# Two attention sweeps woven into two recurrent chains, in a hand-written order

## The chip, the cores and the metric

The kernel runs on one NeuronCore of a Trainium2 chip. The engines are TensorE (PE, with its weight loads PEld), VectorE (DVE), ScalarE (ACT), GpSimd (POOL) and SyncE (SP, which here only issues DMAs). The metric is the device time of one execution in microseconds (us): the median of several runs.

## The reference, cut to what matters

The kernel computes the forward pass and all gradients of a gated sum of two branches for 2048 tokens of width 576.

```python
g = sigmoid((x * gate_w).sum(-1))
out = g * A(x) + (1 - g) * B(x_B)          # and the gradients of out . grad_out

# A: 32 query heads of 18, one key head, full softmax over 2048 x 2048
p = softmax(q_h @ k.T * 18**-0.5); o_h = p @ v;  A = concat(o_h) @ wo

# B: 64 segments of 32 tokens, 32 heads of 128; 8 memory rows go from segment to segment
for s in range(64):
    h = concat(mem, x[32*s:32*s+32])        # 40 rows
    q, k, v = h @ Wq, h @ Wk, h @ Wv
    o = masked_softmax(q @ k.T * 128**-0.5) @ v
    o = o @ Wo
    mem, out_s = o[:8], o[8:]
```

Branch A has no order among its blocks. Branch B's memory rows are a recurrence: 64 steps forward, and 64 steps backward for the gradient.

## The kernel before, in words

The kernel is written in a tile framework: pools hand out buffers ("bufs" is how many a name has), every semaphore is derived from the tiles read and written, and a scheduler orders the instructions by priority. Everything is unrolled. The stages follow each other as `build_full` calls them.

- `prep`, `a_weights`, `a_setup`: gate, transposes of x and of the incoming gradient, branch A's keys and values (tiles KV, VK, WK).
- `a_pass1`, **sweep 1**: for 16 pairs of heads by 4 blocks of 512 queries it makes QD (queries and output gradients of both heads, in the four 32-row strips of one tile; `a_qd`), then runs over 16 key tiles. Per key tile: four matmuls of 32 rows give two scores (a_S) and two dP products (a_dP), ACT takes two exponentials (L947), DVE multiplies both heads' dP by E in one instruction of 1024 columns (L948), and four matmuls with 64 columns of weights add E and W into a_acc. `a_post` normalises a block and keeps its rows of output and dq in SBUF.
- `a_pass2`, **sweep 2**: the same products with keys along the free axis, for 4 blocks of 512 keys by 16 pairs by 16 query tiles; b_acc collects dk and dv with four matmuls of 32 columns each for E and dS.
- `a_out`: branch A's output projection.
- `b_proj_x`: q, k and v of all 2048 tokens, 16 tiles by 3 weights, kept in DRAM as rows and transposed.
- `b_chain_fwd`, **forward chain**: 64 segments. Each projects 8 memory rows with Wk, Wq, Wv (20 matmuls a half of a weight, in four column strips), transposes them, forms the memory rows' scores (c_sm), takes the softmax, multiplies by v (po), and forms the next memory rows with 160 matmuls of 8 columns (c_pm).
- `make_transposed_weights`, then `b_bulk`: everything of B that does not feed the recurrence, 16 token tiles by 8 groups of four heads: scores, softmax, output, dO (five matmuls with WoT and four transposes), dP, dS, dq.
- `b_chain_bwd`, **backward chain**: 64 segments in reverse: dO of the memory rows (r_pj), dS, the gradients of q, k, v (r_pkv, r_pdq), their product with three transposed weights (r_ph, 192 matmuls) and a last reduction to the memory rows' gradient (r_sm, L627).
- `b_post`, `b_mem_tok`, `b_dw`, `a_final`: remaining gradients.

Helpers at L61 to L71 (`evac`, `mm`, `tr`) record all copies out of PSUM, matmuls and transposes, so tiles tell more than lines here. Most DMAs are issued by SP; those of `dq_eng` alternate between SP and POOL.

Of the kernel before, what the change touches and what calls it, by code (L numbers as in the profile page):

```python
# [11 lines left out]
P = 128  # L12

D = 576
# [16 lines left out]
class Kern:  # L31
# [50 lines left out]
    def setup_B_dram(self, dram):  # L82
# [12 lines left out]
        self.xTd = {w: t(w + "xT_dram", [NTT, P, HB, P]) for w in ("q", "k", "v")}  # L95
        self.mTd = {w: t(w + "mT_dram", [NTT, P, HB, 32]) for w in ("k", "v")}
# [6 lines left out]
        self.dsmq_dram = t("dsmq_dram", [NSEG, MEM, HB, 32])  # L103
        self.dmT_dram = t("dmT_dram", [P, NKT, NSEG, MEM])
# [3 lines left out]
    def setup_B_consts(self, pool):  # L108
# [17 lines left out]
        mx = pool.tile([P, 2, 160], BF16, name="maskX")  # L126
        nc.gpsimd.memset(mx[:], 0.0)
        for j in range(2):
            nc.gpsimd.affine_select(out=mx[:, j, 0:128], in_=mx[:, j, 0:128], compare_op=ALU.is_ge, fill=NEGB,
                                    base=0, pattern=[[-1, P]], channel_multiplier=1)  # L130
            nc.gpsimd.memset(mx[:, j, 128:160], NEGB)
            for sl in range(4):
                r = slice(32 * sl, 32 * sl + 32)
                if sl:
                    nc.gpsimd.memset(mx[r, j, 0:32 * sl], NEGB)
                nc.gpsimd.memset(mx[r, j, 128 + 8 * sl:136 + 8 * sl], 0.0)
        self.maskX = mx
# [38 lines left out]
    def b_proj_x(self, sp, psum):  # L176
        nc = self.nc
        for tt in range(self.NTT):
            xt = sp.tile([P, NKT, P], BF16, name="p_x", bufs=2)
            nc.sync.dma_start(xt[:], self.xT_dram[:, :, tt * P:(tt + 1) * P].rearrange("k p t -> p k t"))  # L180
            for w in ("q", "k", "v"):
                tok = sp.tile([P, J], BF16, name="p_tok", bufs=2)
                for jc in range(8):
                    pb = psum.tile([P, 512], F32, name="p_pb", bufs=4)
                    for kt in range(NKT):
                        rows = KT_ROWS[kt]
                        self.mm(pb[:], lhsT=xt[0:rows, kt, :], rhs=self.W[w][0:rows, kt, jc * 512:(jc + 1) * 512],
                                start=(kt == 0), stop=(kt == NKT - 1))
                    self.evac(tok[:, jc * 512:(jc + 1) * 512], pb[:])
                nc.sync.dma_start(self.xtok[w][tt * P:(tt + 1) * P, :], tok[:])  # L190
                tT = sp.tile([P, HB, P], BF16, name="p_tT", bufs=2)
                for h8 in range(4):
                    pt = psum.tile([P, 8, P], BF16, name="p_pt", bufs=2)
                    for i in range(8):
                        h = 8 * h8 + i
                        self.tr(pt[:, i, :], tok[:, h * E:(h + 1) * E], P)
                    self.evac(tT[:, 8 * h8:8 * h8 + 8, :], pt[:])
                nc.sync.dma_start(self.xTd[w][tt], tT[:])
# [7 lines left out]

    def b_chain_fwd(self, keep, sp, psum):
        nc = self.nc
        NSEG = self.NSEG
        hist = keep.tile([P, NKT, NSEG, MEM], BF16, name="memT")  # L210
# [6 lines left out]
        for s in range(NSEG):  # L217
            tt, sl = s // 4, s % 4
            h_ = hm[s % 2]
            kx = sp.tile([P, HB, 32], BF16, name="c_kx", bufs=2)  # L220
            nc.gpsimd.dma_start(kx[:], self.xTd["k"][tt][:, :, 32 * sl:32 * sl + 32])
# [4 lines left out]
            nc.gpsimd.tensor_copy(hist[:, 0:4, s, :], h_[:, 0:4, 0:8])  # L226
            nc.gpsimd.tensor_copy(hist[0:64, 4, s, :], h_[0:64, 4, 0:8])
            if sl == 0:
                mT = {w: sp.tile([P, 4, 8, 4, 8], BF16, name=f"c_{w}mT", bufs=1) for w in ("k", "v")}
            tm = {}  # L230
            for w in ("k", "q", "v"):
                t2 = sp.tile([P, 8, E], BF16, name=f"c_{w}2", bufs=2)
                for j in range(2):
                    pj = psum.tile([P, 512], F32, name="c_pj", bufs=3)
                    for kt in range(NKT):
                        rows = KT_ROWS[kt]
                        for c in range(4):
                            self.mm(pj[32 * c:32 * c + 32, :], lhsT=h_[0:rows, kt, :],
                                    rhs=self.W[w][0:rows, kt, c * 1024 + j * 512:c * 1024 + (j + 1) * 512],
                                    start=(kt == 0), stop=(kt == NKT - 1), tp=(0, 32 * c))  # L240
                    self.evac(t2[:, 4 * j:4 * j + 4, :].rearrange("p u e -> p (u e)"), pj[:])
                tm[w] = t2
                for c in range(4):
                    nc.sync.dma_start(self.mtok[w][s * 8:(s + 1) * 8, c * 1024:(c + 1) * 1024], self.m_rows(t2, c))
                pt = psum.tile([P, 8, P], BF16, name="c_pt", bufs=2)
                for u in range(8):
                    self.tr(pt[:, u, :], t2[:, u, :], P)
                src = pt[:].rearrange("p u (c t) -> p u c t", t=32)[:, :, :, 0:8]
                if w == "q":
# [1033 lines left out]
```

## Time and profile before

| what | value |
|---|---|
| median of 3 runs | 11392.89 us (11385.8 to 11398.63) |
| profiled execution, its own time | 11406.79 us |
| span in the profile | 11405.0 us |
| PE busy | 8865.9 us, 78% |
| DVE, ACT, POOL busy | 36%, 31%, 14% |
| mean granted PE clock | 0.725 |

A span is from the first to the last instruction. "Busy" is the time in which an engine had an instruction; PE's ends are modelled, and a busy PE is not PE at its peak. The granted clock is the share of full speed at which the throttle lets PE run. In the timeline the columns are start, length, engine, line, operation, output<-inputs, shape and count, and in brackets the idle time before and what ended it. In groups by line or tile: count, then either busy time and mean ns, or shortest, median and longest ns.

### The profile page before, as it was taken

The numbers are of one execution on the slowest core, as the hardware profiler recorded it, in microseconds if no ns is written. First come the engines' busy times: TensorE is split into PE (matmuls) and PEld (weight loads), VectorE is DVE, ScalarE is ACT, GpSimd is POOL, SyncE is SP. The second block draws the span as 40 slices with busy tenths as digits, with TensorE's granted clock in tenths as the row PEclk, the third lists the DMA queues.
The fourth block names the chain that finished last, engine by engine and source line by source line (L and its number), as shares of the span: only waits on it lengthen the run. The fifth ranks groups of instructions, "written<-read, shape, count | busy, mean of one in ns | idle before, by whom it ended". The sixth has DMA issues, their size and how long they took to land. (4 is left out here: it accounts for less than half of the span.)

```text
span 11405.0 us, 219104 instructions
## 1 busy us (share of the span) xinstructions
PE 8865.9 (78%) x91009; PEld 3869.9 (34%) x91416; DVE 4143.1 (36%) x5742; ACT 3592.5 (31%) x6629; POOL 1540.5 (14%) x2664
## 2 busy tenths in 40 slices
PE   6777777799999998888876666665777776655898
PEld 2222222211112444444443333333333333333344
DVE  5666666688886331212122222221111111111001
ACT  4666666677776331111121111110000001112000
POOL 2111111100000000000022222221111111112101
PEclk8888888655556997777755655666666668877999
DMA  1000000311112442222254444444222224445544
GB/s 66 9 9 9 9 9 9 96 49 49 46 49 85 175 172 43 44 44 43 43 164 114 111 118 114 111 117 121 55 55 54 55 60 125 124 116 188 169 149 137
DMA packets 929961, 945.24 MB, mean 83 GB/s; under 512 B 457193, under 2 KB 801458, under 8 KB 910146
## 3 DMA queue, kind: packets, MB, share of 16 engines
q1 hardware_dynamic: 859330, 714.18, 21.7%
q0 software_dynamic: 69632, 217.01, 6.9%
q8 instruction: 716, 11.73, 0.4%
q14 instruction: 283, 2.32, 0.1%
HBM read 558.16 MB, written 372.57 MB: 82 GB/s over the span
## 5 line engine op out<-in xcount | busy, mean ns | idle before, releaser
L948 DVE TENSOR_TENSOR a_W<-a_dP,a_E 128x1024 bf16<-128x1024 f32 x1024 | 1252.4, 1225 | 583.3 <-ACT a_E L947 483.8
L1035 DVE TENSOR_TENSOR b_dS<-b_dP,b_E 128x1024 bf16<-128x1024 f32 x1024 | 1231.3, 1223 | 211.3 <-PE b_S L66 163.1
L947 ACT ACTIVATE a_E<-a_S 128x512 bf16<-128x512 f32 x2048 | 1116.0, 595 | 445.8 <-PE a_S L66 385.6
L1034 ACT ACTIVATE b_E<-b_S 128x512 bf16<-128x512 f32 x2048 | 1111.1, 594 | 351.0 <-DVE b_dS L1035 243.2
L66 PE MATMUL b_S<-b_KV,b_QD 32*128 32x512 bf16 x2048 | 897.8, 588 | 25.0 <-DMA b_QD<-qd_dram 25.0
L66 PE MATMUL a_acc<-a_W,a_WK 128*64 128x512 bf16 x2048 | 471.0, 447 | 387.5 <-DVE a_W L948 387.1
L66 PE MATMUL b_acc<-b_E,b_SD 128*32 128x512 bf16 x2048 | 626.9, 608 | 4.3 <-DMA b_SD<-sd_dram 3.3
L66 PE MATMUL b_acc<-b_dS,b_SD 128*32 128x512 bf16 x2048 | 626.2, 607 | 4.3 <-DVE b_dS L1035 1.8
L66 PE MATMUL b_dP<-b_KV,b_QD 32*128 32x512 bf16 x2048 | 620.7, 603 | 0.0
L66 PE MATMUL r_ph<-WT,r_dT 128*32 128x512 bf16 x12288 | 562.0, 353 | 29.5 <-ACT r_dT L608 29.5
L66 PE MATMUL a_S<-a_QD,a_KV 32*128 32x512 bf16 x2048 | 539.4, 443 | 44.6 <-ACT a_QD L922 43.1
L66 PE MATMUL w_acc<-w_d,w_h 128*128 128x512 bf16 (+1 forms) x2352 | 523.1, 380 | 37.5 <-DMA w_d<-dqx_dram 34.8
L66 PE MATMUL a_acc<-a_E,a_VK 128*64 128x512 bf16 x2048 | 520.2, 441 | 28.9 <-ACT a_E L947 25.8
L679 DVE COPY y_T<-y_pt 128x512 bf16<-128x512 bf16 x384 | 151.3, 422 | 934.8 <-PE y_pt L71 920.5
L66 PE MATMUL a_dP<-a_QD,a_KV 32*128 32x512 bf16 x2048 | 455.6, 441 | 0.0
L66 PE MATMUL y_pdx<-WT,y_T 128*128 128x64 bf16 (+1 forms) x2976 | 426.5, 289 | 24.1 <-ACT y_dx L685 10.9
L66 PEld LDWEIGHTS <-a_WK 128*64 128x64 bf16 x2048 | 195.1, 111 | 687.5 <-issue 680.0
L66 PE MATMUL c_pm<-c_oT,WoN 128*128 128x8 bf16 (+1 forms) x10080 | 340.3, 173 | 38.4 <-DVE c_oT L282 27.0
L66 PEld LDWEIGHTS <-r_dT 128*32 128x32 bf16 x12288 | 256.4, 109 | 334.9 <-issue 217.6
L66 PEld LDWEIGHTS <-b_SD 128*32 128x32 bf16 x4096 | 120.6, 101 | 731.1 <-issue 725.5
L66 PEld LDWEIGHTS <-WoN 128*128 128x128 bf16 (+1 forms) x10080 | 338.1, 114 | 50.9 <-issue 49.6
L66 PE MATMUL y_pk<-y_qB,y_dsB 128*128 128x512 bf16 x112 | 49.9, 446 | 391.9 <-DMA y_dsB<-dsmq_dram 391.9
(424 smaller groups left out, 13336.7 us busy)
## 6 DMA issues: line engine op xcount, KB each, us to landing
b_SD<-sd_dram SPq DMA_DIRECT2D x64, 512.0 KB
b_QD<-qd_dram SPq DMA_DIRECT2D x64, 512.0 KB
qx_dram<-p_tok SPq DMA_DIRECT2D x16, 1024.0 KB
qxT_dram<-p_tT SPq DMA_DIRECT2D x16, 1024.0 KB
kx_dram<-p_tok SPq DMA_DIRECT2D x16, 1024.0 KB
kxT_dram<-p_tT SPq DMA_DIRECT2D x16, 1024.0 KB
vx_dram<-p_tok SPq DMA_DIRECT2D x16, 1024.0 KB
vxT_dram<-p_tT SPq DMA_DIRECT2D x16, 1024.0 KB
```

Of the source, the lines that this page charges most:

```text
L66: return self.nc.tensor.matmul(out, lhsT, rhs, start=start, stop=stop, tile_position=tp, skip_group_check=True)
L679: nc.vector.tensor_copy(tT[:], pt[:])
L947: nc.scalar.activation(Et[:, i, :], S[i][:, :], ACT.Exp, scale=SCALEA)
L948: nc.vector.tensor_tensor(out=Wt[:], in0=dP[:], in1=Et[:], op=ALU.mult)
L1034: nc.scalar.activation(Et[:, i, :], S[i][:, :], ACT.Exp, scale=SCALEA)
L1035: nc.vector.tensor_tensor(out=dS[:], in0=dP[:], in1=Et[:], op=ALU.mult)
```

## The change

Both sweeps and both chains become generators. `weave` runs one piece of a chain and then two half-steps of a sweep, with a context in which the written order is kept on every engine. A half-step is one head's share of a key tile: 2048 in each sweep. Sweep 1 goes with the forward chain, sweep 2 with the backward chain.

Inside the sweeps, scores run two half-steps ahead of their use, and the DVE product is 512 columns wide. QD is made by `a_qd_all` ahead of the weave and read back from DRAM block by block, as are KV, VK and WK. `a_post` is cut into steps, uses the chain's PSUM slot and writes its rows to DRAM at once. The chains' copies out of PSUM after projections are all ACT's, the transposed copies DVE's; their loads are issued by SP a segment ahead; c_x and r_x are single PSUM slots shared by the chain's small products; the backward product r_ph is cut into two halves of 288 columns. dO of the tokens moves from `b_bulk` into `b_proj_x`, which `b_bulk` then loads, and WoT is made earlier. The memory rows go to DRAM in each segment and are turned to token order in `b_mem_tok`.

The core of the diff:

```diff
+    def weave(self, chain, sweep, per_piece):
+        with self.tc.manual_schedule():
+            for _ in chain:
+                for _ in range(per_piece):
+                    next(sweep, None)
+            for _ in sweep:
+                pass
 ...
-    def b_proj_x(self, sp, psum):
+    def b_proj_x(self, ws, srcT, sp, psum):
 ...
-            for w in ("q", "k", "v"):
+            for w in ws:
+                Wt = self.WoT if w == "dO" else self.W[w]
 ...
+    def proj_mem(self, st, Wt, j, psum, tag):
+        pj = psum.tile([P, 512], F32, name=tag, bufs=2)
+        for kt in range(NKT):
+            rows = KT_ROWS[kt]
+            for c in range(4):
+                self.mm(pj[32 * c:32 * c + 32, :], lhsT=st[0:rows, kt, :],
+                        rhs=Wt[0:rows, kt, c * 1024 + j * 512:c * 1024 + (j + 1) * 512],
+                        start=(kt == 0), stop=(kt == NKT - 1), tp=(0, 32 * c))
+        return pj
 ...
     def b_chain_fwd(self, keep, sp, psum):
+            nxt = load(s + 1)
+            for w in ("k", "q"):
                 for j in range(2):
+                    pj = self.proj_mem(h_, self.W[w], j, psum, "c_pj")
+                    self.evac(flat(t2[w], j), pj[:], use="s")
+                    yield
+            src = self.mem_T(t2["k"], psum, "c_x", 1)
+            mT_out("k", src)
+            rows_out("k")
+            yield
+            pj = self.proj_mem(h_, self.W["v"], 0, psum, "c_pj")
 ...
+            ps = psum.tile([P, P], F32, name="c_x", bufs=1)
 ...
             nc.scalar.activation(Et[:].rearrange("p a b -> p (a b)"), ps[:], ACT.Exp, scale=SCALEB)
+            yield
+            src = self.mem_T(t2["v"], psum, "c_pj", 2)
+            mT_out("v", src)
+            yield
+            den = psum.tile([P, 64], F32, name="c_x", bufs=1)
 ...
             self.expand(PB[:], pn[:].rearrange("p a (u q) -> p (a u) q", q=8), 16)
+            yield
+            yield
+            po = psum.tile([P, 8, 32], F32, name="c_x", bufs=1)
 ...
+            yield
             if s + 1 < NSEG:
+                pm = psum.tile([P, NKT, 8], F32, name="c_x", bufs=1)
                 for kt in range(NKT):
 ...
+                    if kt == 1:
+                        yield
+                    if kt == 3:
+                        yield
 ...
     def b_bulk(self, keep, wp, sp, psum):
+                dO_g = sp.tile([P, 512], BF16, name="x_dO", bufs=3)
+                self.dq_eng().dma_start(dO_g[:], self.xtok["dO"][trows, gc])
+                dOT = sp.tile([P, 512], BF16, name="x_dOT", bufs=3)
+                self.dq_eng().dma_start(dOT[:], self.xTd["dO"][tt][:, 4 * g:4 * g + 4, :].rearrange("p h t -> p (h t)"))
 ...
-                pd = psum.tile([P, 512], F32, name="x_po", bufs=2)
-                for kt in range(NKT):
 ...
-                transp4(dO_g, dOT[:])
 ...
     def b_chain_bwd(self, keep, sp, psum):
+            for hf in range(2):
+                lo, hi = 288 * hf, 288 * hf + 288
+                ph = psum.tile([P, 288], F32, name="r_pj", bufs=2)
                 for wi in (2, 0, 1):
 ...
+                    if wi != 1:
+                        yield
+                nc.scalar.copy(hs[:, lo:hi], ph[:])
 ...
+    def a_qd_all(self, sp, psum):
+        for p in range(NPR):
+            for qb in range(self.T // 512):
+                self.a_qd(p, qb, sp, psum)
 ...
+    def a_pass1(self, keep, sp, psum, xps):
+        def ex(m):
+            E_[m] = sp.tile([P, 512], BF16, name="a_E", bufs=5)
+            nc.scalar.activation(E_[m][:], S.pop(m)[:, :], ACT.Exp, scale=SCALEA)
 ...
+        for m in range(M + 2):
 ...
+                if m + 2 < M:
+                    mm_S(m + 2)
+                dP = psum.tile([P, 512], F32, name="a_dP", bufs=2)
+                r = slice(64 + 32 * i, 96 + 32 * i)
+                self.mm(dP[:, :], lhsT=self.KV[r, kt * P:kt * P + P], rhs=QD[b][r, :], tp=(64 + 32 * i, 0))
+                if m + 2 < M:
+                    ex(m + 2)
+                W_[m] = sp.tile([P, 512], BF16, name="a_W", bufs=4)
+                nc.vector.tensor_tensor(out=W_[m][:], in0=dP[:], in1=E_[m][:], op=ALU.mult)
+            if m % 2 == 1:
 ...
+                    acc_mm(acc, n - 1, W_, self.WK, False, n % 16 == 0)
 ...
+                        acc_mm(acc, n, E_, self.VK, False, False)
+            elif post is not None:
+                if next(post, "end") == "end":
+                    post = None
+            yield
 ...
+                k.a_qd_all(a1s, a1p)
 ...
+                k.weave(k.b_chain_fwd(a2k, cfs, cfp), k.a_pass1(a2k, a2s, a2p, cfp), 2)
 ...
+                k.weave(k.b_chain_bwd(rk, rs, rp), k.a_pass2(a3k, a3s, a3p), 2)
```

`a_pass2` has the same form: S of half-step m+2, dP and the DVE product of half-step m, and after each odd half-step four b_acc matmuls for the key tile before. `load(b + 2)` in `a_pass1` reads a block's QD two blocks ahead; in `a_pass2` QD and SD come in chunks of four query tiles, two ahead.

More of the change, by code (lines that the diff above doesn't have):

```diff
@@ L610, in b_chain_bwd @@
+                self.mm(pkv[:, 0, u, :], lhsT=mrow["q"][:, u, :], rhs=f(dSqB[:, u]), start=False, stop=True)
             nc.scalar.copy(dT[:, 1], pkv[:, 0])
             nc.sync.dma_start(self.dTm_dram[s // 16][:, :, s % 16, :], dT[:].rearrange("p w u c -> p w (u c)"))
[L612 to L613 removed]
+            if s:
+                nxt = load(s - 1)
+            yield
+            hs = sp.tile([P, D], F32, name="r_hs", bufs=1)
```

638 lines of the change are left out of this document (345 added, 293 removed).

## The prediction

> **What bounds the kernel now.** The page gives a chain of waits spread over all stages, so I cut the span at the stages' first and last instructions and read the windows. Columns: stretch, its length, busy time of PE, weight loads, DVE, ACT, POOL, granted clock, DMA share, GB/s.
>
> ```profile
> 108.50:2168.00 2059.50, 1486.02 (x9424) 468.20 (x9423) 1265.44 (x1088) 1299.55 (x2373) 303.10 (x817) 0.83 0.04 12
> 2168.00:3613.00 1445.00, 1434.15 (x8192) 254.56 (x8192) 1231.47 (x1026) 1112.76 (x2052) 8.39 (x14) 0.50 0.18 57
> 3659.70:4252.00 592.30, 581.78 (x3396) 242.02 (x3464) 199.23 (x288) 209.66 (x288) 2.34 (x3) 1.00 0.45 181
> 4252.00:5719.00 1467.00, 1258.14 (x24628) 693.36 (x24624) 291.31 (x642) 166.39 (x387) 132.55 (x190) 0.75 0.25 45
> 5810.00:7783.00 1973.00, 1322.48 (x9745) 725.16 (x9889) 502.80 (x1025) 360.96 (x656) 518.20 (x647) 0.60 0.42 116
> 7783.00:9370.00 1587.00, 1155.14 (x23748) 602.93 (x23748) 303.87 (x898) 116.36 (x320) 190.89 (x343) 0.64 0.29 64
> ```
>
> In order: sweep 1, sweep 2, x projections, forward chain, bulk, backward chain. Sweep 1 loads DVE and ACT for some 1270 and 1300 of 2060 us; the chains load them for a fifth of the time at most and need PE, which then waits for one small product after another. Nothing runs beside either, because the stages follow each other. Sweep plus chain is 3526.5 us and 3032 us, 55.1 and 47.4 us for each of 64 segments.
>
> The clock decides what PE can take. In the timeline of sweep 1, a cold iteration, then a hot one:
>
> ```profile
> 1001.49 0.10 PEld L66 LDWEIGHTS <-a_KV 32*128 32x128 bf16 x3 [0.81 <-issue]
> 1002.03 0.64 PE L66 MATMUL a_acc<-a_W,a_WK 128*64 128x512 bf16 x2
> 1002.46 0.64 PE L66 MATMUL a_acc<-a_E,a_VK 128*64 128x512 bf16 x2
> 1003.02 0.10 PEld L66 LDWEIGHTS <-a_KV 32*128 32x128 bf16 x4 [0.81 <-issue]
> ...
> 1016.32 0.41 PE L66 MATMUL a_acc<-a_W,a_WK 128*64 128x512 bf16 x2 [0.55 <-DVE a_W L948]
> 1016.54 0.41 PE L66 MATMUL a_acc<-a_E,a_VK 128*64 128x512 bf16 x2
> 1016.87 0.10 PEld L66 LDWEIGHTS <-a_KV 32*128 32x128 bf16 x4 [0.41 <-issue]
> 1017.20 0.11 PEld L66 LDWEIGHTS <-a_WK 128*64 128x64 bf16 x1 [0.23 <-issue]
> 1017.70 0.41 PE L66 MATMUL a_acc<-a_W,a_WK 128*64 128x512 bf16 x2 [0.43 <-DVE a_W L948]
> ```
>
> Ends overlap in these rows, so the starts tell the cost. A full array over 512 columns (call it a unit) takes 0.22 us hot (16.32 to 16.54) and 0.43 cold (02.03 to 02.46); a change of tile shape adds 0.11 (16.54 to 16.87 is 0.33). The four S and dP matmuls run side by side as one unit. The sweep of one key tile for two heads (an iteration) so needs 0.33+0.22+0.33 = 0.88 us of PE hot, 1.53 cold, and hot it waits for DVE (period 1.38).
>
> Sweep 1 hot uses 3 units, 0.65 of 1.38 us: array share 0.47, clock stays up. Sweep 2 uses 2 units, 0.43 of 1445/1024 = 1.41 us: share 0.31, clock 0.50 for the whole stage, though PE is busy 99%. In the forward chain, PE line by line and one window:
>
> ```profile
> 4993.40 0.40 PE L71 MATMUL c_pt<-identB,c_k 128*128 128x128 bf16 x4
> 4993.73 2.24 PE L66 MATMUL c_pj<-Wq,hm 128*32 128x512 bf16 x31
> ...
> 5004.39 5.35 PE L66 MATMUL c_pm<-c_oT,WoN 128*128 128x8 bf16 x160 [0.42 <-DVE c_oT L282]
> 5010.09 4.30 PE L66 MATMUL c_pj<-Wk,hm 128*32 128x512 bf16 x40 [0.35 <-DVE hm L295]
> ```
>
> ```profile
> 5004.40:5009.80 5.40, 5.34 (x160) 5.23 (x159) 0.00 (x0) 0.00 (x0) 0.00 (x0) 0.50 0.65 96
> ```
>
> 160 matmuls of 8 columns keep PE busy 5.34 of 5.40 us and the clock is 0.50: it follows array share, not PE's busy time. Between 0.31 and 0.47 I place the bound at 0.35. [...]
>
> **The change, part by part.** Both sweeps go in half-steps of one head (2048 each), two behind each chain piece, in program order on every engine. PE work adds up; DVE and ACT work lies beside it. A piece with its two half-steps therefore costs the largest of its engines' sums; buffers are two half-steps deep, so idle time of one piece is not lent to the next, and I add up the largest, not the averages.
>
> A pair of half-steps: PE stays 0.88 hot (both halves' S and dP still adjoin), plus 0.11 for the shape change from the chain. DVE now has two 512-column products for one of 1024:
>
> ```profile
> L948 DVE TENSOR_TENSOR a_W<-a_dP,a_E 128x1024 bf16<-128x1024 f32 x1024 | 1252.4, 1225 | 583.3 <-ACT a_E L947 483.8
> L947 ACT ACTIVATE a_E<-a_S 128x512 bf16<-128x512 f32 x2048 | 1116.0, 595 | 445.8 <-PE a_S L66 385.6
> ```
>
> ```profile
> L61 DVE CAST p_tok<-p_pb x192: 690/692/692, 3662.4 to 4248.3; 128x512 bf16<-128x512 f32 x192
> ```
>
> No 512-column product is in the trace; between half of 1225 (0.61) and the same-sized cast (0.69) I take 0.69, since each instruction has its start. So DVE 1.38, ACT 1.19 a pair.
>
> Forward segment, hot, in us. Six projection pieces: 20 matmuls of 2.24/31 are 1.40, +0.99 = 2.39 (ACT 1.78). Three transposing pieces: four transposes start 0.33 before what follows, so eight are 0.66, +0.99; DVE with a 0.29 copy 1.67 is a little more. Scores: for 65 matmuls of 8 columns I take 0.75, between nothing and c_pm's 0.033 each (2.1), as their weights are a quarter as wide: 1.74. The softmax piece is DVE's:
>
> ```profile
> 5001.73 0.56 DVE L270 RECIPROCAL c_rd<-c_sm 128x64 f32<-128x64 f32 x1 [0.76 <-PE c_sm L66]
> 5002.38 0.29 DVE L272 TENSOR_TENSOR c_pn<-c_E,c_rd 128x128 bf16<-128x128 bf16 x1
> 5002.71 0.42 DVE L201 TENSOR_TENSOR c_PB<-c_pn,bmask 128x512 bf16<-128x512 bf16 x1
> 5003.91 0.42 DVE L282 CAST c_oT<-c_sm 128x256 bf16<-128x256 f32 x1 [0.78 <-PE c_sm L66]
> ```
>
> The first three make 1.38+1.27 = 2.65. The empty piece is 1.38, po 1.80 (DVE, with the fourth row's copy), pm in three pieces of 64, 64 and 32 matmuls at 5.35/160 = 0.033: 3.13, 3.13, 2.06. Sum 35.2, plus 1.1 of PE for a_post's eight transposes: 36.3.
>
> Array time (columns by the used part of the array, at the hot unit's rate) is 0.64 a pair, 0.96 a projection, 0.43 a transposing piece: about 19 us, share 0.5 over the segment, but 0.27 in the three pm pieces (0.85 in 3.13). So I expect the clock to fall there and rise during the next projections: cold for 2.5 pairs (0.65 each), all of the first projection piece (0.65+0.7, since 4.30/40 makes 2.15) and half of the second (0.7), and 0.5 for segments where softmax already drops it: +4.2. 40.5 us by 64 is 2592, with 20 to start and drain 2612. Bounds: 2343 never cold (36.3), 3270 always cold: 16 pairs at 1.64, six projections at 2.15 and 12 us of the rest make 51.
>
> QD is now made ahead of the weave, 64 blocks in which the five pairs of projections, Abs, correction and copy overlap across three PSUM tiles; in sweep 1 they stood in a row:
>
> ```profile
> 1024.42 0.64 PE L66 MATMUL a_S<-xT,a_wqp 128*64 128x512 bf16 x1
> ...
> 1027.59 0.37 PE L66 MATMUL a_S<-a_absq,a_smneg 64*64 64x512 bf16 x1 [0.69 <-ACT a_absq L919]
> ```
>
> Between six hot units (1.3) and the 3.2 us seen here, I take 1.6, being pipelined and dense: +100.
>
> Backward segment. A pair needs 2 units with 2 shape changes, 0.66 hot, 1.10 cold. From the chain's timeline and sweep 2's:
>
> ```profile
> 8499.54 5.86 PE L66 MATMUL r_ph<-WT,r_dT 128*32 128x512 bf16 x164
> 8506.03 1.28 PE L66 MATMUL r_sm<-selF,r_hs 128*128 128x8 f32 x10 [0.63 <-DVE r_hs L620]
> 8516.36 0.40 DVE L541 STREAM_TRANSPOSE r_pxq<-r_pxpad 128x256 bf16<-128x256 bf16 x1
> ```
>
> ```profile
> 2800.07 0.11 PEld L66 LDWEIGHTS <-b_SD 128*32 128x32 bf16 x4 [0.66 <-issue]
> 2800.61 0.11 PEld L66 LDWEIGHTS <-b_QD 32*128 32x128 bf16 x4 [0.44 <-issue]
> ```
>
> (From 00.07 to 00.61 is a cold group with its shape change, 0.54; two make 1.10.) Two projections 2.17 each; then DVE-bound pieces 2.65, 2.10, 2.23 (products 1.38 plus copies, transposes at 0.40 and expansions); two of ACT, 1.57 each; six ph pieces of 32 matmuls over 288 columns, at 0.034 each 1.1, +0.77 = 1.87, 0.3 more where two transposes fall in; pm 1.28+0.77; an empty one 1.38. Sum 29.4. Shares are near 0.33 from piece 3 to 7, so the clock drops, costs little beneath DVE there and 2.0 in the first ph pieces, with 1.3 elsewhere: 32.7, by 64 is 2093. The backward chain yields only 15 pieces, so 130 half-steps trail: 130 x 0.69 = 90. With weight loading as before (50) and 20 to start: 2253. Bounds: 2042 never cold; 2720 always cold, where 15 pairs at 1.2, projections at 2.15, ph pieces at 8 x 0.24 and 6 us of the rest make 40.
>
> dO moves from bulk to a projection pass: a third of 592.3, +197. The projection weights' load waits until dO's weights leave SBUF; before, it lay beneath sweep 2. First matrix exposed: +25 (0 to 60). Bulk loses five matmuls, four transposes and two copies a group:
>
> ```profile
> L66 PE MATMUL x_po<-WoT,x_dbT 128*128 128x512 bf16 (+1 forms) x512 | 285.0, 614 | 28.1 <-issue 27.9 <-DMA x_kmT<-kmT_dram 0.2
> L438 POOL TENSOR_TENSOR x_prod<-x_dOT,x_oTa 128x512 bf16<-128x512 bf16 x128 | 146.6, 1145 | 460.8 <-DVE x_dOT L414 421.4 <-DMA ox_dram<-x_o 20.3 <-DMA px_dram<-x_P 15.9
> ```
>
> Their place is taken by the wait for o's copy, its transposes and POOL's 1.15 us product, so of 285 us and 128 x 0.5 for transposes I take 300 off (50 to 345). Two more loads a group add an issue each on SP and POOL, both idle most of bulk. The chains' loads move from POOL's queue to SP:
>
> ```profile
> 8499.92 0.31 SPq L524 DMA_DIRECT2D r_kx<-kx_dram  x1
> ```
>
> Some 26 issues a forward and 45 a backward segment, at 0.31 and little between, are under half of SP's time. SP also waits in order: behind a write of rows that waits for ACT, or a_post's three writes that wait for POOL, stand the sweep's loads and the next segment's. These are issued a whole segment, or two of the sweep's blocks, before use, so I count nothing; if that cover is gone, each segment pays the late part, a few us, which the stall rival holds. Moved transposes of weights cancel. A hand-over between engines at each of 31 pieces a segment, 0.05 us (0 to 0.2): +100.
>
> The profiled run took 11406.79 us (span 11405.0). 11406.8 - 3526.5 + 2612 + 100 - 3032 + 2253 + 197 + 25 - 300 + 100 = 9835; the median stands 14 below that run, so **9820 us**.
>
> **The rivals.**
>
> All hot: sweeps fill the gaps and the clock never falls. 9820 - 269 - 211 = 9340 us. For it: average shares of 0.5. Against: the pm window. [...]
>
> Cold throughout, as in sweep 2: 9820 + 658 + 467 = 10945 us. For it: a weave that runs long has a lower share, and feeds itself; shares in half of the pieces are near 0.33. Against: projections at 0.6, which opened the clock in the chain.
>
> Slower: PE, in order, meets each chain piece before its input exists, because DVE and ACT have the sweep's two products ahead of it, and each piece costs PE plus DVE instead of the larger. That is about 34+26 us forward (DVE: 16 pairs at 1.38 and 4 of its own), 24+25 backward: 3840 and 3130+160, with the other terms (+222, less handovers' 100) about 12000 us. It decides from 0.8 us a piece (1587 us over 1984 pieces). For it: chain results share one PSUM slot (c_x, r_x), and dP has two buffers. Against: consumers stand one piece behind producers except at po, pm and dn, where two half-steps cover them.
>
> **How the numbers follow.** Alternating clock 0.52, all hot 0.17, cold 0.20, in-order stalls 0.09, and 0.02 that gains and stalls cancel. Own range of the likeliest: 9500 to 10250. The range 9300 to 10800 reaches into hot and cold and leaves the stalls out. No change is within 0.2%, about what a measurement can tell. Faster 0.9, same 0.01, slower 0.09.
>
> **What would show it.** Right: weave 1 near 2600 us, weave 2 near 2200, clock between 0.7 and 0.9 with 0.50 during c_pm, PE busy over 85%, a 512-column a_W near 0.69 us, bulk near 1670. Wrong: clock 0.50 throughout, PE's idle time before chain matmuls put down to DVE or ACT, a load of W under which PE stands, or a bulk that keeps 1970.

## The result and the profile after

The changed kernel takes 9585.96 us (median of 4 runs, 9568.68 to 9601.77) against 11391.24 us before (median of 4, one run more than in the table above): a ratio of 0.8415, 95% interval [0.8399, 0.843]. The profiled execution took 9568.68 us, with a span of 9566.9 us and a mean granted clock of 0.819 (before: 11405.0 us and 0.725).

The windows of the changed kernel, cut at its stages, with the columns of the prediction's first fence. In order: QD ahead, the dO pass, the wait for the projection weights, the first weave, what lies between it and bulk, bulk, the second weave with its weight load, its tail of half-steps without a chain, and `b_post`.

```profile
108.50:242.00 133.50, 128.43 (x714) 38.98 (x711) 45.05 (x69) 37.02 (x64) 19.68 (x35) 0.97 0.22 75
265.00:465.00 200.00, 190.46 (x1130) 90.31 (x1152) 54.73 (x129) 75.31 (x129) 8.54 (x16) 0.99 0.48 186
465.00:500.00 35.00, 17.82 (x72) 7.28 (x74) 3.40 (x8) 4.40 (x8) 3.69 (x7) 0.60 0.96 329
1160.00:3625.00 2465.00, 2368.19 (x33308) 1028.32 (x33309) 1512.98 (x2751) 1407.41 (x2686) 254.10 (x706) 0.87 0.22 37
3625.00:3713.00 88.00, 40.90 (x256) 19.14 (x259) 11.31 (x25) 14.84 (x30) 12.41 (x27) 0.70 0.28 79
3713.00:5391.00 1678.00, 951.67 (x8619) 578.38 (x8732) 459.50 (x888) 281.79 (x527) 591.91 (x780) 0.63 0.52 139
5391.00:7463.00 2072.00, 1891.63 (x31458) 861.80 (x31454) 1442.32 (x2766) 1217.46 (x2378) 68.59 (x212) 0.82 0.37 81
7463.00:7560.00 97.00, 96.98 (x498) 19.80 (x495) 79.35 (x124) 66.19 (x122) 9.46 (x11) 0.50 0.22 62
7560.00:8603.00 1043.00, 639.60 (x5785) 374.33 (x5896) 152.06 (x386) 160.84 (x273) 167.15 (x314) 0.81 0.43 124
```

The two pairs of sweep and chain, 3526.5 and 3032 us one after the other, are now 2465 and 2169. Both weaves keep PE over 90% busy, with DVE at 61 and 70%, ACT at 57 and 59%.

The two smaller stages that the sum took as unchanged, in the windows of the kernel before:

```profile
3613.00:3659.70 46.70, 36.17 (x237) 16.42 (x242) 10.34 (x24) 12.29 (x25) 8.15 (x15) 0.88 0.37 116
9370.00:10455.00 1085.00, 645.94 (x5789) 377.81 (x5902) 151.48 (x385) 161.03 (x274) 171.66 (x323) 0.80 0.42 122
```

What lies between sweep and the next stage went from 46.7 to 88 us, and `b_post` from 1085 to 1043.

The clock within one segment of the first weave: PE's timeline of the changed kernel, then three windows of the same segment.

```profile
2011.70 1.75 PE L66 MATMUL c_x<-c_oT,WoN 128*128 128x8 bf16 x64
2013.38 0.38 PE L66 MATMUL a_S<-a_QD,l_KV 32*128 32x512 bf16 x1
...
2014.26 1.78 PE L66 MATMUL c_x<-c_oT,WoN 128*128 128x8 bf16 x64
2015.97 0.60 PE L66 MATMUL a_S<-a_QD,l_KV 32*128 32x512 bf16 x1
...
2020.71 2.18 PE L66 MATMUL c_pj<-Wk,hm 128*32 128x512 bf16 x20
...
2023.48 1.37 PE L66 MATMUL c_pj<-Wk,hm 128*32 128x512 bf16 x20
```

```profile
2012.15:2015.56 3.41, 3.41 (x113) 2.75 (x110) 1.77 (x3) 1.26 (x3) 0.00 (x0) 1.00 0.97 110
2015.56:2022.39 6.83, 6.83 (x83) 3.39 (x79) 2.83 (x6) 2.17 (x4) 0.00 (x0) 0.50 0.20 37
2022.39:2049.70 27.31, 25.91 (x347) 9.91 (x344) 19.07 (x35) 18.61 (x36) 3.92 (x11) 1.00 0.12 27
```

64 small c_pm matmuls take 1.68 us until the sweep's next row starts (2011.70 to 2013.38), 0.026 each. The first of these windows is PE busy 3.41 of 3.41 us, and the clock falls right behind it, through the first projection (2.18 us) and up again before the second (1.37). In array time that window holds one pair of three units (0.64 us) and some 100 matmuls of 8 columns at 0.0033 us, 0.97 of 3.41: a share of 0.28, an estimate from the hot unit of 0.22 us.

The DVE products of both sweeps in the page of the changed kernel:

```profile
L1052 DVE TENSOR_TENSOR a_W<-a_dP,a_E 128x512 bf16<-128x512 f32 x2048 | 1328.3, 686 | 797.3 <-PE a_dP L66 757.3
L1185 DVE TENSOR_TENSOR b_dS<-b_dP,b_E 128x512 bf16<-128x512 f32 x2048 | 1313.6, 684 | 611.9 <-PE b_dP L66 509.1
```

DVE waits for PE, not the other way round; 686 ns is the 0.69 us that the prediction took from a cast.

Waits of the second weave, in the changed kernel: total, times, longest; first those of PE and its weight loads, then those of SP's queue.

```profile
PEld L66 <- DMA b_QD<-qd_dram: 127.6, 73, 26.3
PE b_S L66 <- DMA b_QD<-qd_dram: 92.8, 34, 25.8
```

```profile
SPq L648 <- ACT r_dT L647: 240.9, 63, 7.3
SPq L1146 <- PE b_acc L66: 150.6, 102, 2.4
SPq L1144 <- PE b_dP L66: 140.2, 77, 4.2
```

A wait that the sum had counted as nothing: a load of QD, late. One wait in each of the first two rows, 26.3 and 25.8 us, is the start of the weave, where the first tiles are loaded; the others recur through the segments.

### The profile page after: what moved, and what is told of

It reads as the page before. It is cut to its first block, busy times and chain, and to the rows that moved or that the text cites. A ratio compares the mean times of both kernels' runs of the same rounds, so it can differ in the third digit from the quotient of the medians.

```text
span 9566.9 us, 226296 instructions
## 1 busy us (share of the span) xinstructions
PE 7831.6 (82%) x91018; PEld 3772.5 (39%) x91416; DVE 4114.3 (43%) x7885; ACT 3642.1 (38%) x6854; POOL 1360.6 (14%) x2452
## 5 line engine op out<-in xcount | busy, mean ns | idle before, releaser
L1052 DVE TENSOR_TENSOR a_W<-a_dP,a_E 128x512 bf16<-128x512 f32 x2048 | 1328.3, 686 | 797.3 <-PE a_dP L66 757.3
L1185 DVE TENSOR_TENSOR b_dS<-b_dP,b_E 128x512 bf16<-128x512 f32 x2048 | 1313.6, 684 | 611.9 <-PE b_dP L66 509.1
L66 PE MATMUL b_S<-b_KV,b_QD 32*128 32x512 bf16 x2048 | 550.4, 446 | 116.0 <-DMA b_QD<-qd_dram 92.8
L66 PE MATMUL a_dP<-a_QD,l_KV 32*128 32x512 bf16 x2048 | 590.9, 424 | 49.9 <-DVE a_W L1052 49.9
L66 PE MATMUL a_S<-a_QD,l_KV 32*128 32x512 bf16 x2048 | 560.7, 424 | 8.7 <-DMA a_QD<-qd_dram 8.0
L66 PE MATMUL r_pj<-WT,r_dT 128*32 128x288 bf16 x12288 | 497.7, 309 | 0.0
L63 ACT CAST p_tok<-p_pb 128x512 bf16<-128x512 f32 x512 | 299.5, 586 | 514.1 <-PE p_pb L66 514.1
L66 PE MATMUL a_acc<-a_E,l_VK 128*64 128x512 bf16 x2048 | 443.4, 429 | 24.3 <-DVE a_acs L1060 24.3
L66 PE MATMUL a_acc<-a_W,l_WK 128*64 128x512 bf16 x2048 | 462.5, 448 | 0.0
L66 PE MATMUL y_pdx<-WT,y_T 128*128 128x512 bf16 (+1 forms) x2977 | 422.3, 287 | 23.1 <-ACT y_dx L737 10.9
```

The costliest lines, as they stand in the source:

```text
L63: nc.scalar.copy(out, in_)
L66: return self.nc.tensor.matmul(out, lhsT, rhs, start=start, stop=stop, tile_position=tp, skip_group_check=True)
L1052: nc.vector.tensor_tensor(out=W_[m][:], in0=dP[:], in1=E_[m][:], op=ALU.mult)
L1185: nc.vector.tensor_tensor(out=D_[m][:], in0=dP[:], in1=E_[m][:], op=ALU.mult)
```

## The experiments

My theory: PE's sum sets the weaves; overlap is what gains; the clock follows the share of array work in a window, and c_pm and the DVE-bound pieces cost time by dropping it; QD's loads are late because SP issues in order. The rivals are given with each run.

**Overlap, or the rewritten stages?** The weave runs the whole chain, then the whole sweep.

```diff
             for _ in chain:
-                for _ in range(per_piece):
-                    next(sweep, None)
+                pass
             for _ in sweep:
                 pass
```

> Same instructions as the changed kernel, but each chain runs whole before its sweep, so no chain piece lies beside a half-step. Theory A (the gain is overlap: a segment's chain and its 16 pairs lie beside each other): the stages add up again. Forward chain as before, 22.9 us a segment, 1465 us; sweep 1 alone at DVE's two products of 686 ns a pair, 1.4 us, 1024 pairs, 1430, and up to 60 for a_post; backward chain 23.8 us a segment, 1520; sweep 2 alone 1.4 us a pair, 1430. Instead of 2465 and 2169 us that is about 2950 and 2950, and a total near 10850 us (10700 to 11100). Theory B (the gain is the rewritten sweep, with scores two half-steps ahead and QD made before, and the overlap is worth little): the total stays under 10000 us. In the windows A shows PE busy below 90% in the forward chain and the sweep's DVE over 90% busy.

Measured: 11037.65 us, ratio to before 0.9691 [0.9669, 0.9713]. The windows of this run: forward chain, sweep 1, backward chain, sweep 2.

```profile
1170.00:2480.00 1310.00, 1152.96 (x24608) 688.07 (x24609) 175.12 (x576) 242.53 (x448) 5.95 (x12) 0.75 0.32 50
2484.00:4364.00 1880.00, 1799.36 (x8695) 415.51 (x8693) 1359.23 (x2174) 1200.97 (x2237) 246.23 (x693) 0.63 0.06 14
6152.00:7393.00 1241.00, 940.25 (x23739) 651.87 (x23739) 247.53 (x830) 197.16 (x448) 58.04 (x202) 0.85 0.41 79
7400.00:9013.00 1613.00, 1611.97 (x8192) 330.20 (x8192) 1319.74 (x2048) 1112.62 (x2051) 7.21 (x10) 0.50 0.14 44
```

So 11037.65 - 9585.96 = 1452 us of the gain comes from running the two side by side, what that does to the clock included, and some 350 from the rewriting. The total is within theory A, but not by its parts. The chains alone got faster (1467 to 1310, 1587 to 1241). The sweeps alone are far from DVE's 1.4 us a pair: 1.84 and 1.58, at clocks of 0.63 and 0.50, with DVE busy only 72% and 82%. Sweep 2 in half-steps is slower alone than it was before (1445). Woven, the clocks are 0.87 and 0.82: the chain's matmuls do a second service, they raise the clock for the sweep.

**Does the clock follow array share?** c_pm streams 32 columns, 24 of them never read.

```diff
-                pm = psum.tile([P, NKT, 8], F32, name="c_x", bufs=1)
+                pm = psum.tile([P, NKT, 32], F32, name="c_x", bufs=1)
+                oF = oT[:].rearrange("p u c q -> p (u c q)")
 ...
+                        st = 32 * (h % 8) + 8 * (h // 8)
+                        wd = 32 if st + 32 <= 256 else 8
-                        self.mm(pm[0:ncols, kt, :], ..., rhs=oT[:, h % 8, h // 8, :], ...)
+                        self.mm(pm[0:ncols, kt, 0:wd], ..., rhs=oF[:, st:st + wd], ...)
```

> The 160 matmuls of c_pm stream 32 columns instead of 8; the 24 added columns are never read. In the changed kernel 64 of them start 0.026 us apart when the clock is high, so the added columns cost little issue time but raise the array share of the window (0.28 in the one before the drop). Theory A (the clock follows the share of array work in a window): the two cold windows in each forward segment go, the first projection piece falls from 2.18 to 1.4 us, and the weave falls from 37.5 us a segment by about 1.9, some 120 us in all: 9440 to 9500 us, mean clock of the weave from 0.87 to above 0.95. Theory B (the clock follows whether PE is busy at all, or the drop comes from elsewhere, since PE is busy in both): no change of the clock, and 32 columns cost at most what they stream, 0 to 30 us more: 9580 to 9620 us.

Measured: 9401.19 us, 185 less than the changed kernel. The window of the first weave, and c_pm with the first projection in the timeline:

```profile
1167.00:3444.00 2277.00, 2176.89 (x33304) 962.56 (x33304) 1511.90 (x2750) 1406.32 (x2685) 252.87 (x705) 0.96 0.23 40
```

```profile
2023.62 1.78 PE L66 MATMUL c_x<-c_oT,WoN 128*128 128x32 bf16 x64
2026.22 1.75 PE L66 MATMUL c_x<-c_oT,WoN 128*128 128x32 bf16 x64
2028.69 1.15 PE L66 MATMUL c_x<-c_oT,WoN 128*64 128x32 bf16 x32
2030.65 1.37 PE L66 MATMUL c_pj<-Wk,hm 128*32 128x512 bf16 x20
```

More useless work made the kernel faster: the same issue time per matmul (64 start to end in 1.75 to 1.78 us with either width), clock 0.87 to 0.96, first projection 2.18 to 1.37. Theory A in kind; what went was worth 188/64 = 2.9 us a segment, more than the 1.9 expected, and at 0.96 some of the cold time is still there.

**Why are QD's loads late?** They go to POOL's queue.

```diff
-                nc.sync.dma_start(QD[:], self.qd_dram[p][:, q4 * 512:(q4 + 1) * 512])
+                nc.gpsimd.dma_start(QD[:], self.qd_dram[p][:, q4 * 512:(q4 + 1) * 512])
 ... (the same for SD)
```

> In sweep 2 the loads of QD and SD are issued on POOL's queue instead of SP's. In the changed kernel PE and its weight loads wait 67 and 98 us for b_QD in the second weave, while SP's queue stands 241 us behind r_dT and 138 and 114 us behind sweep 2's own buffers. Theory A (SP works in order, and loads of QD stand behind a store that waits for ACT): the waits for b_QD go, and the second weave falls by 60 to 95 us, to about 2090. Theory B (the load is late because its buffer comes free late, or the DMA itself takes that long): the waits stay, and the time within 20 us of the changed kernel's. Theory C (POOL's queue is worse, because there the loads stand behind POOL's own products): 20 us or more slower.

Measured: 9498.42 us, 88 less. The second weave's window and waits, those of POOL and PE's weight loads, of PE, and of SP's queue:

```profile
5417.00:7385.00 1968.00, 1860.58 (x31391) 859.55 (x31392) 1430.86 (x2744) 1209.33 (x2367) 306.01 (x684) 0.84 0.38 83
```

```profile
POOL b_QD L1144 <- PE b_dP L66: 1176.7, 233, 44.2
...
PEld L66 <- DMA b_QD<-qd_dram: 1.2, 2, 0.7
```

```profile
PE b_S L66 <- DMA b_KV<-kv_dram: 26.3, 1, 26.3
```

```profile
SPq L648 <- ACT r_dT L647: 513.1, 64, 9.3
```

The wait falls from 127.6 to 1.2 us: theory A. (The 26 us at the start of the weave stay, now put down to b_KV; the waits that went are the recurring ones.) SP now stands even longer behind r_dT, and PE does not wait for it, because only the next segment's loads are behind it. These are 24 loads, issued right behind that store, most at some 0.3 us each (in the changed kernel from 6509.89 to 6521.79 us in one segment), so in the changed kernel QD's loads could stand behind the store, behind the 24, or both; the run takes them away from both and does not separate the two.

**What was the move of dO worth?** dO is computed in bulk again.

```diff
-                with PS("pdp") as pdp:
-                    k.b_proj_x(("dO",), k.dbT_dram, pds, pdp)
 ...
+                pd = psum.tile([P, 512], F32, name="x_po", bufs=2)
+                for kt in range(NKT): ...
+                dO_g = sp.tile([P, 512], BF16, name="x_dO", bufs=3)
+                nc.scalar.copy(dO_g[:], pd[:])
 ...
+                transp4(dO_g, dOT[:])
```

> dO is computed in the bulk stage again, as before the change, and the pass that makes it ahead of the first weave is left out; WoT is made in the bulk stage. Theory A (the term 'dO moved', by the windows: bulk 1973 to 1678, pass 200 us, exposed weight load 35 us; the move gained 60): bulk back at about 1970 us, total about 60 us longer than the changed kernel, 9620 to 9670. Theory B (bulk became shorter for another reason, such as the earlier transposes of WoT or other DMA traffic, and the move itself lost): bulk stays under 1800, and the total falls by 100 us or more.

Measured: 9667.68 us, 82 longer; bulk is back:

```profile
3535.00:5475.00 1940.00, 1349.31 (x9825) 724.89 (x9826) 498.17 (x1013) 359.35 (x654) 507.95 (x632) 0.59 0.41 112
```

1940 against 1678 is 262 for the dO work in bulk, 193 less ahead of the weave, and 24 more between weave and bulk (112 for 88). Theory A.

**Do the two gains add?** Both edits, no others.

> The two edits of e2_pm32 and e3_qd_pool together. They act in different weaves: 32 columns took 185 us from the first (2277 for 2461 us), the other queue 78 from the second. If the causes are independent, as the theories have it (array share there, SP's order here), the gains add: 9586 - 185 - 88 = 9313 us, 9300 to 9330. If one of them had gained by something common, such as less DMA traffic at the same time, the sum is smaller: above 9350.

Measured: 9315.64 us, where 9313 was expected. The gains add, as independent causes would have it.

**Can the second weave be kept hot?** On top of both, useless matmuls at four pieces of a backward segment.

```diff
+        def filler(n):
+            fj = psum.tile([P, 512], F32, name="r_pj", bufs=2)
+            for i in range(n):
+                self.mm(fj[:], lhsT=self.zeros[:], rhs=self.WoT[:, 0, 0:512])
 ...
             self.expand(PqB[:], pq[:, :, 0:8], 8)
+            filler(2)
             yield
 ... (the same behind dSB, the dq copy and dn)
```

> e6_both with eight useless matmuls of 512 columns with zero weights in each backward segment, two each at the transposing piece, the scores, the dq product and the empty piece, into a PSUM tile that nothing reads. They cost PE 8 x 0.22 = 1.8 us a segment when the clock is high, 113 us in all. In the second weave windows with an array share near 0.3 precede each drop of the clock, in pieces where DVE's two products and copies last longer than PE's work. Theory A (clock by array share, and the filler lies in PE's idle time under DVE): the drops go, clock of the second weave from 0.84 to above 0.93, and a segment falls from 29.9 us by 1 to 2 us: 60 to 130 us less than e6_both. Theory B (the filler raises the share, but PE has no idle time there, so that its own cost eats the gain): clock up, time within 40 us of e6_both. Theory C (no hold on the clock): clock the same, 100 us or so longer.

Measured: 9261.96 us, 54 less than with both edits. The second weave with both edits, then with the filler:

```profile
5235.00:7198.00 1963.00, 1856.56 (x31396) 859.03 (x31388) 1430.25 (x2745) 1210.27 (x2368) 305.88 (x684) 0.85 0.38 83
```

```profile
5230.00:7146.00 1916.00, 1814.68 (x31929) 857.99 (x31930) 1431.06 (x2750) 1204.82 (x2372) 306.66 (x686) 0.94 0.39 86
```

The clock rises as in A, from 0.85 to 0.94, but the gain lies just below A's range. The window is 47 us shorter although PE does some 113 us of useless products in it; how much of these lies under cover of other engines, and how much the clock pays back, is not separated. The four runs go from 9252.63 to 9316.0 us, so this gain is less sure than the others: the intervals of the two ratios to before, [0.8101, 0.8148] and [0.8149, 0.8176], only just do not meet.

**Does order matter, or only the sums?** Two chain pieces, then four half-steps, on the changed kernel.

```diff
-            for _ in chain:
-                for _ in range(per_piece):
+            for i, _ in enumerate(chain):
+                for _ in range(2 * per_piece * (i % 2)):
                     next(sweep, None)
```

> The changed kernel with the weave twice as coarse: two chain pieces in a row, then four half-steps. The same instructions in another order. Theory A (what keeps the in-order stalls away is that every chain result has two half-steps to arrive): pieces that now follow each other at once meet their input late, by about a copy and two hand-overs (1 to 1.5 us); with 8 such places a segment in the first weave and 7 in the second that is 8 x 64 x 1.2 = 600 and 550 us, less some that do not depend on each other: 10000 to 10800 us, with PE waiting for ACT and DVE tiles of the chains. Theory B (the engines' sums set the time, whatever the order, and the hand-overs cost): half of the hand-overs go, 0 to 100 us faster, 9480 to 9590.

Measured: 10317.83 us, 732 longer than the changed kernel: theory A's time, but by another way. Its first and second weave:

```profile
1175.00:4019.00 2844.00, 2575.50 (x33303) 1059.21 (x33304) 1518.39 (x2750) 1407.73 (x2685) 253.69 (x705) 0.81 0.18 32
5811.00:8196.00 2385.00, 2110.19 (x31384) 967.74 (x31376) 1443.37 (x2742) 1223.56 (x2364) 59.48 (x200) 0.80 0.31 69
```

Of 379 us in the first weave PE's idle time explains 172 (268.5 for 96.8) and longer busy time 207; in the second 94 of 313. What PE waits for, in the first weave and then in the second:

```profile
PE a_acc L66 <- DVE a_acs L1060: 109.5, 63, 1.7
...
PE a_S L66 <- ACT a_E L1018: 40.7, 131, 0.7
PE c_x L66 <- DVE c_oT L316: 32.9, 63, 0.5
```

```profile
PE b_S L66 <- ACT b_E L1164: 129.3, 350, 1.0
```

Theory A has PE wait for tiles of the chains. It does so for 33 us in the first weave (c_oT) and for some 24 in the second (r_dOT 12.2, r_dOm 11.4): late chain results are a small part of 692 us. The waits that grew are for tiles of the sweeps themselves: a_acs from 24.3 to 109.5, a_E from 0.7 to 40.7, b_E from 15.6 to 129.3. Counted from the start of each PE matmul to the start of the next, the sweeps' matmuls take 353 us more in the first weave and 320 in the second, the chains' only 29 more and about the same. So order matters, but where it costs is the sweep: four half-steps in a row outrun buffers that are two half-steps deep and go at the pace of ACT and DVE, which two chain pieces in a row then leave idle. This is read from the waits; no run with deeper buffers tests it. The clock fell too, from 0.87 to 0.81 and from 0.82 to 0.80, and what share of the longer rows is the clock's stays open.

**More columns still?** Up to 64 in c_pm, on top of both edits: the width of the tile and of the slice, `wd = min(64, 256 - st)`.

> e6_both with up to 64 columns in c_pm in place of 32. With 32 columns the clock of the first weave is 0.96: one window in about five segments, three in some, still falls below a share near 0.33. 64 columns last 0.027 us at the high clock, as long as the 0.026 between the starts of c_pm's matmuls. Theory A (share decides): the last drops go, clock of the first weave above 0.98, and about 0.5 us a segment, 30 us in all, less than e6_both. Theory B (a matmul that must stream 64 columns is no longer free): 160 x 0.005 to 0.02 us a segment are added, 50 to 200 us longer than e6_both.

Measured: 9428.08 us, 112 longer than with both edits. The QD stage, which the edit does not touch, and the first weave, then two c_pm rows of different segments:

```profile
108.00:245.00 137.00, 136.54 (x531) 34.43 (x529) 32.97 (x51) 26.76 (x47) 12.47 (x23) 0.61 0.14 47
...
1205.00:3563.00 2358.00, 2264.57 (x33303) 1034.25 (x33304) 1513.06 (x2750) 1406.30 (x2685) 253.53 (x705) 0.94 0.23 39
```

```profile
2002.48 1.97 PE L66 MATMUL c_x<-c_oT,WoN 128*128 128x64 bf16 x64
...
2035.24 2.99 PE L66 MATMUL c_x<-c_oT,WoN 128*128 128x64 bf16 x64
```

64 columns are no longer free: 1.97 for 1.75 us by 2.5 groups by 64 is 35 us (theory B), and 2.99 in a group that starts at half clock (the two a_acc rows before it start 0.42 us apart). The first weave is 78 us longer than with 32 columns (2358 for 2280); the 43 beyond these 35 go with the clock, 0.94 for 0.96, and with the cold groups. The clock is not higher because another drop remains, in the softmax and empty pieces before po: those a_acc rows, behind them, are the first cold ones of the segment, and with useless products in these two pieces the last run below reaches 0.99. The rest of the 112 us, some 40, has nothing to do with c_pm: it is the QD stage, whose window has a clock of 0.61 where it was 0.94 with both edits, and which ended at 283 us against 243. Why it stayed cold is open, and the four runs of this kernel spread from 9412.65 to 9456.35 us.

**The remaining drop.** On top of the filler kernel: two useless matmuls each in the softmax and the empty piece, and the stores of the deltas spread over two queues and more buffers.

```diff
             self.expand(PB[:], pn[:].rearrange("p a (u q) -> p (a u) q", q=8), 16)
+            filler(2)
             yield
+            filler(2)
             yield
 ...
-            dlT = sp.tile([64, 512], BF16, name="a_dlT", tag="a_qt", bufs=1)
+            dlT = sp.tile([64, 512], BF16, name="a_dlT", tag="a_E", bufs=5)
 ...
-                    nc.sync.dma_start(self.qd_dram[p][...], dlT[...])
+                    (nc.sync if i else nc.gpsimd).dma_start(self.qd_dram[p][...], dlT[...])
```

> e5_fill with two more edits in separate stages. First, two useless 512-column matmuls each in the softmax piece and the empty piece of a forward segment, where DVE is the longer engine and windows with an array share of 0.32 to 0.37 still drop the clock in about two segments of three. Theory A (share decides, and the filler lies in PE's idle time): clock of the first weave from 0.96 to above 0.98, 35.4 us a segment to 34.6 to 35.0, 25 to 50 us less. Theory B (no idle time is left there): 4 x 0.22 x 64 = 56 us are added. Second, the 128 stores of the deltas after the first weave go in turns to SP's and POOL's queue, from more than one buffer; in the changed kernel PE stands there three times for 10.7 us behind the stores of one buffer. If the stores of 0.33 us each on one queue are the cause, the gap between the last a_W and the first bulk product shrinks from some 110 us by about 20; if the transfers themselves are, by nothing. Together 9190 to 9225 us against 9262 of e5_fill; by theory B and no effect of the queues, about 9320.

Measured: 9211.74 us, 50 less; ratio to before 0.8081 [0.807, 0.8092], the best kernel of this study. The two kernels were measured at different times, against medians of 11395 and 11412 us for the kernel before, so some 14 of the 50 may be that; the two windows below are 41 and 15 us shorter. The first weave:

```profile
1167.00:3405.00 2238.00, 2168.12 (x33576) 959.16 (x33577) 1511.61 (x2752) 1401.76 (x2690) 256.04 (x714) 0.99 0.24 41
```

The clock is 0.99, theory A: 2238 us for 2279, and 34.7 a segment. The gap behind the weave shows its cause in the timelines, PE's and SP's of the changed kernel and PE's of this one:

```profile
3632.95 0.58 PE L71 MATMUL c_x<-identB,a_dl 128*64 128x128 bf16 x4 [5.24 <-ACT a_dlT L1080]
3644.24 0.58 PE L71 MATMUL c_x<-identB,a_dl 128*64 128x128 bf16 x4 [10.70 <-ACT a_dlT L1080]
```

```profile
3632.93 31.94 SPq L1083 DMA_DIRECT2D qd_dram<-a_dlT  x96
```

```profile
3404.36 0.59 PE L71 MATMUL c_x<-identB,a_dl 128*64 128x128 bf16 x4 [0.67 <-ACT a_dlT L1099]
```

10.7 us is 32 stores of one buffer at SP's 0.33 each (31.94/96); with five buffers and two queues PE waits 0.67. Which of the two edits did it is not separated. The way from the last a_W to the first bulk product fell from 109.1 to 93.7 us, 15 where 20 were expected: now PE waits 12.1 us for `a_out`'s load of branch A's rows.

## Why the prediction was right

Forecast 9820 us, measured 9586, inside the likeliest case's own range, and the case is the one that came: a clock that alternates within each segment. Of its signs of being wrong only one shows, and small: PE stands for 30 us under the loads of Wk and Wv before the projections of x and for 27 under WoT at the start of the second weave, where the sum had 25 and, for weight loading, 50. Against the profiled spans:

| term | predicted, us | measured, us |
|---|---|---|
| first weave | 2612 | 2465 |
| QD ahead | +100 | +133.5 |
| second weave with tail | 2253 | 2169 |
| dO pass, exposed weight load | +197, +25 | +200, +35 |
| bulk | -300 | -295 |
| hand-overs | +100 | nothing left for them |
| gap behind the first weave | 0 | +41 |
| `b_post` | 0 | -42 |

Terms were too high by 373 us (147, 100, 84, 42) and too low by 92 (33, 13, 5, 41), so that the total came out 2.4% off is in part luck.

The largest errors, term by term:

- **First weave, -147.** The segment takes 38.2 us ((2465 - 20)/64) for the 40.5 of the sum. With the clock held up, in the last run, it takes 34.7, so the hot pieces (36.3) were priced 1.6 too high, 102 us. Of these 72 are c_pm, whose matmuls start 0.026 us apart, not the 0.033 taken from the chain before, where the clock was 0.50: 160 x 0.007 x 64. The cold surcharge is 3.5 us a segment, not 4.2: 45 us. The 0.9 us of filler in the last run blurs this split: as far as they are not under cover, the hot price is lower still and the surcharge higher. That the clock falls in c_pm and rises in the next projections was right.
- **Hand-overs, 100 to nothing.** The 34.7 us of the last run hold 0.9 us of filler and lie below the 36.3 that the sum had for hot pieces without hand-overs. With c_pm at 0.026 the sum is 35.2, and no 0.05 a piece is left in it, unless other pieces were priced too high by as much; no run separates the two. The 0.05 was the author's estimate, near the 0.06 us of one hand-over in the rows of the kernel before (c_oT's copy ends at 5004.33, c_pm starts at 5004.39); no run shows it as a cost of each piece.
- **Second weave, -84, two errors against each other.** SP's in-order loads, counted as nothing "issued a whole segment, or two of the sweep's blocks, before use", cost some 90 us (the run with QD's and SD's on POOL's queue is 88 shorter): they stand behind the store of r_dT, the 24 loads that follow it, or both, and chunks of four query tiles come too soon after each other for that. (The prediction has the chains' loads move to SP's queue; in the kernel before, only one load a segment in each chain, c_kx and r_vxT, was on POOL's, and the row that it shows is SP's.) The segment itself was over-priced: from one r_dT store to the next it is 31.2 us on average in the changed kernel, 29.9 with the loads on POOL's queue and 29.0 with the filler and a clock of 0.94, for a hot sum of 29.4 and 32.7 with the surcharge. So the surcharge above all was too large.
- **QD, +33.** 133.5/64 is 2.1 us a block for the 1.6 taken between 1.3 and 3.2, at a clock of 0.97.
- **The gap, +41, a step that was not in the sum.** The last block's `a_post` and the deltas' rows have no half-step above them any more, and 32 stores a buffer go out on one queue. **`b_post`, -42,** was not foreseen and not tested.
- **dO and bulk** came as worked out; undoing them alone costs 82 us (by the terms: 300 - 197 - 25 = 78).
- **A slip.** The stall rival's "other terms (+222, less handovers' 100)" are 122 (100 + 197 + 25 - 300 + 100), less 100; its 12000 comes out with these.

The rivals. All hot was 9340 us: no run of the changed kernel is there, but with the clock kept up on purpose the first weave alone comes to 2238 for its bound of 2343. Cold throughout didn't come, but its price was too low: sweep 2 alone and cold takes 1.58 us a pair, not 1.10. The in-order stalls did not come: in the changed kernel PE waits for no tile of the chains for more than 12 us in all (dm, once, at the start of the second weave). The rival's own price, 1.1 us at each of 1984 pieces (12000 - 9820), is far from what was seen even in the coarser weave, where chain pieces follow each other at once and PE waits some 57 us in all for their tiles. The bound of the clock's share, placed at 0.35, lies among the shares of 0.30 to 0.40 that the weaves show with both outcomes, as counted below.

## What to carry to other kernels

When two stages are woven, add up PE's work piece by piece, and by the share of the array that it uses, not only by whether PE is busy: here 3.41 us of mostly small matmuls that kept PE busy all through were followed by a clock of 0.50 for 1.00, and widening them from 8 to 32 columns at the same issue time gained 185 us; useless products in pieces where another engine is the longer one gained 54 us in the second weave and about 41 in the first. Weave finely: twice as coarse cost 732 us here, and the waits suggest that a run of one stage that is longer than its buffers are deep goes at the pace of its slowest engine, and the other stage cannot make up for it. In a fixed order, keep a load off a queue with stores that wait for a compute engine: here that gained 88 us.

## What the runs showed of the hardware that was not expected

In the traces of the kernel before and of the changed kernel the granted clock has two values, 1.00 and 0.50, and its 621 and 591 changes lie on one grid of 3.41 us in each, within 0.02 us. What the clock did behind a stretch of that grid went with the array share of the stretch. The shares are estimates: each matmul row counts with its columns at the granted rate (0.22 us for 512 when hot, twice that at half clock) times the part of the array that it uses, spread from its start to its modelled end. In the first weave of the changed kernel, from 1300 to 3600 us, all 59 hot stretches with a share under 0.32 were followed by half clock, 12 of the 36 between 0.35 and 0.40, and none of the 410 above 0.40. From half clock it rose behind all 71 stretches that used 0.79 or more of the array's time at that clock, and behind none of the 98 under 0.72. Sweep 1 alone, in the first experiment, ran at 0.63 on average; its three units a pair, 3 x 0.43 us of 1.84, fill 0.70 at half clock, under all the shares behind which the weave's clock rose. Woven with the chain's projections the clock rose 71 times in those 2300 us, in which there are some 61 segments of 37.9 us.

The shares at which it fell are about the same elsewhere: in the second weave of that kernel, from 5450 to 7460 us, behind all 76 hot stretches under 0.30, 36 of 40 between 0.30 and 0.36, and none of the 274 above 0.38. Those at which it rose are not: in its bulk stage the clock rose behind 31 of 62 half-clock stretches with shares of 0.62 to 0.70, in the two weaves behind none of 12 and none of 27. So these counts hold for the weaves, and what exactly decides stays open.

A woven segment also falls into step with these stretches: in the changed kernel, from one first projection to the next, segments of 37.4, 37.5, 37.5, 39.7 and 39.0 us follow each other over and over from the sixth on, together 191.2 us, which is 56 of them.
